# One schedule as written for the whole kernel, other PSUM banks for the turns, and a block's last products in two halves of the columns

## The chip, the cores and the metric

The kernel runs on one NeuronCore of a Trainium2 chip. Its time is device microseconds (us) of one execution; a kernel's time is the median of several. The engines are named as in the profile: PE is TensorE (PEld its weight loads), DVE VectorE, ACT ScalarE, POOL GpSimd, SP SyncE; a name with q (PEq, DVEq) is the engine's instruction queue, in which branches and loads of registers are handled. All products are matmuls on TensorE that write into PSUM, a memory of eight banks.

## The reference

Three steps follow one another. First, attention inside chunks of 64 positions, for 2 × 576 = 1152 tokens and 8 heads of 64. Second, a mixture of 8 experts in which every token goes to one expert and an expert takes at most 288 tokens. Third, a dense mixture of 4 domains.

```python
idx = argmax(x @ w_gate); gate = softmax(x @ w_gate)[idx]
# tokens of expert e in order, the first 288 kept
h = maximum(disp[e] @ w1[e], 0); y = h @ w2[e]     # 512 -> 1024 -> 512
out[i] = gate[i] * y[expert(i), place(i)]          # 0 where not kept
# dense: for each of 4 domains
out += p[:, e:e+1] * (maximum(x @ w1[e], 0) @ w2[e])
```

How many tokens an expert gets depends on the inputs; with these, six experts have tokens.

## The kernel before

**Stages.** Up to about 60 us: attention in nine tiles of 128 tokens, with the gate and the counting of places. From 60 to 240 us: the experts. From 240 to 602 us: the dense mixture. Each fp32 value is split into a high and a low part that TensorE takes at full rate; a product of two such is three matmuls (high·high, low·high, high·low; `PAIRS`). In the profile `hl` is a weight's two parts (ScalarE casts the high part, L115, VectorE subtracts to get the low one, L119), `xt` those of the tokens, `ht` those of the hidden layer.

**An expert.** The numbers that tell how many tokens each expert has are made on VectorE into the tile `ovi` at the end of attention, `gidx` holds the token numbers for the gathers, and `over` (L447) the surplus of each expert, on VectorE too. `over` is the last operation that reads the PSUM tile `n_ps`; the next stage's tiles take over the banks of attention. An expert's tokens are worked in up to three blocks, `wins`: block 0 (tokens 0 to 127), block 1 (128 to 255) and block 2, the small one, of 64 tokens. `form` says which of them are executed: 1 block 0, 2 blocks 0 and 2, 4 blocks 0 and 1, 3 all three. On every engine the blocks 1 and 2 stand in `tc.If` (L677, L682, L683), so each engine compares a register and branches. The order in an expert is block 1, the small block, block 0, and in block 0 the next expert's tokens are turned and its weights split (`also`).

With these inputs the order is, in us of the profile: first expert block 1 (from 67.9) and block 0; second block 1 (from 100.5), small block (114.7 to 126.2) and block 0; third block 0 alone (from 141.8); fourth small block (158.6 to 174.2) and block 0; fifth small block (189.6 to 206.7) and block 0; sixth block 0 alone (from 222.3).

**A block** (`block`): `first(h)` multiplies tokens by one half of `w1` into the bank `pg0[w]` or `pg1`; ScalarE copies it out (`hs`); `turn(h)` transposes it on TensorE into a tile `tp` (L580, in a small block L578); ScalarE and VectorE make `ht` of it, L596 the high and L597 the low part; `second(h)` multiplies `ht` by `w2` into `y` (L574). At the end ScalarE copies `y` to `yr` in two halves of 256 columns (L627), TensorE turns `yr` into another `tp`, and the result is split into `x2` for the dense stage. `xprep` turns the next expert's gathered tokens (L540), `xprep_small` those of its small block (L545).

**What sets the order.** In `tc.manual_schedule` an engine issues its instructions as the code is written; outside, a scheduler orders them. Before, attention is under one such context for all engines, the expert stage and the dense stage each under one of their own for four engines, and the code between them under none. A tile named `tp` comes from a pool tag of two banks that rotate (`bufs=2`): whoever writes into a bank waits for its last reader, and where that reader stands in a `tc.If`, for the engine to have passed the branch.

**Numbers in registers.** `numbers` reads values of `ovi` into a register of each engine (a `TENSOR_LOAD` in its queue, L549). Before, this happens once, ahead of the expert stage: nine values on every engine, eight more on ScalarE and VectorE.

Of the kernel before, what the change touches and what calls it, by code (L numbers as in the profile page):

```python
# [9 lines left out]
F32 = mybir.dt.float32  # L10
# [8 lines left out]
ENG = mybir.EngineType  # L19

P = 128
NTOK = 1152
# [49 lines left out]
def kernel(ctx: ExitStack, tc: tile.TileContext, kqv_d, wg, w_all, dp, cst, out, cap):  # L72
# [4 lines left out]
    assert cap <= XW  # L77

    dpool = ctx.enter_context(tc.tile_pool(name="dpool", bufs=1, space=DRAM))
    x_d = dpool.tile([NTOK, DM], F32, name="x_d")  # L80
# [44 lines left out]
    with ExitStack() as ast:  # L125
        ap_ = ast.enter_context(tc.tile_pool(name="attn", bufs=2))
        ps = ast.enter_context(tc.tile_pool(name="aps", bufs=1, space=PSUM))
        ast.enter_context(tc.manual_schedule())

# [387 lines left out]
    def w2(h, part, ff):  # L517
        return hls[2 * h + 1][:, part, ff * DM:(ff + 1) * DM]

    with ExitStack() as est, tc.manual_schedule(engines={ENG.PE, ENG.Activation, ENG.DVE, ENG.SP}):  # L520
        hp_ = est.enter_context(tc.tile_pool(name="mh", bufs=2))
        xtp = est.enter_context(tc.tile_pool(name="mx", bufs=1))
        ps = est.enter_context(tc.tile_pool(name="mps", bufs=1, space=PSUM))

        ys2 = [ps.tile([P, DM], F32, name=f"y{j}") for j in range(2)]


        pg0 = [ps.tile([P, FH], F32, name=f"pg0{j}") for j in range(3)]
        pg1 = ps.tile([P, FH], F32, name="pg1")
        xts = [xt0, xtp.tile([P, 2 * KD * XW], F32R, name="xt1")]  # L530
        xbig = [x[:, 0:4 * KD * P].rearrange("p (a k n) -> p a k n", a=2, k=KD) for x in xts]
# [16 lines left out]
        def numbers(src, **kw):  # L548
            return nc.values_load_multi_w_load_instructions(src, min_val=0, **kw)[1]  # L549

        kept, *form_r = numbers(ovi[0:1, 0:1 + NE], max_val=NTOK)
        o_r = numbers(ovi[0:1, 1 + NE:1 + 2 * NE], engines=(ENG.Activation, ENG.DVE), max_val=NTOK)
        regs = []
# [6 lines left out]
        def block(k, w, also=()):  # L560
# [4 lines left out]
            both = n < P  # L565
            y = ys2[w % 2]
            hs, ht = {}, {}
            pg = (pg0[w], pg1)

            def products(o, t, wt, start, stop):  # L570

                pairs = ((0, 0), (0, 1)) if both else PAIRS
                for i, (a, b) in enumerate(pairs):
                    nc.tensor.matmul(o, t(a), wt(b), start=start and i == 0, stop=stop and i == len(pairs) - 1)  # L574

# [15 lines left out]
            def turn(h):  # L591
                tp = ps.tile([P, NF, n], F32, tag="tp", bufs=2, name="tp")
                for j in range(NF):
                    turned(tp[:, j], hs[h][:, j * P:j * P + P])
                ht[h] = hp_.tile([P, NF, 2, n], F32R, tag="h", name="ht")
                nc.scalar.activation(out=ht[h][:, :, 0], in_=tp, func=ACTF.Relu)  # L596
                nc.vector.scalar_tensor_tensor(out=ht[h][:, :, 1], in0=tp, scalar=0.0, in1=ht[h][:, :, 0].bitcast(F32),  # L597
                                               op0=ALU.max, op1=ALU.subtract)

            def second(h, ffs):  # L600
                for j in ffs:
                    products(y, lambda a: ht[h][:, j].rearrange("p a n -> p (a n)") if both else ht[h][:, j, a],
                             lambda b: w2(h, b, j), h == 0 and j == 0, h == NH - 1 and j == NF - 1)

# [17 lines left out]
            place(4)  # L622
            second(1, range(NF))
            yr = hp_.tile([P, DM], F32, tag="ys", bufs=1, name="yr")
            ty = ps.tile([P, KD, n], F32, tag="tp", bufs=2, name="tp")
            for j in range(2):
                nc.scalar.copy(yr[:, j * 256:j * 256 + 256], y[:, j * 256:j * 256 + 256])  # L627
            place(5)
# [22 lines left out]
        def expert(k):  # L651
# [3 lines left out]
            if k == 0:  # L655
# [6 lines left out]
                for kd in range(KD):  # L662
                    xprep(0, kd, ps.tile([P, 512], F32, tag="tp", bufs=2, name="tp") if kd < 2 else (pg0[0], pg1)[kd - 2])
                for h in range(2):
# [9 lines left out]
            elif k + 2 < NE:  # L674
                gather(k + 2)
            late(k)
            with tc.If(form_r[k] > 2):  # L677
                block(k, 1)
# [20 lines left out]
            def nxt(i, kd):  # L699
                if k + 1 < NE:  # L700
                    t = pg1 if len(turns) == KD else pg0[1 + len(turns) % 2]
                    turns.append(t)
                    also[i].append(lambda: xprep(k + 1, kd, t) if kd < KD else xprep_small(k + 1, t))
# [19 lines left out]
            block(k, 0, also)  # L723
            if k == 0:
                scatter(meta_d, [(posi[:, i:i + 1], meta[:, i]) for i in range(NT)], [])
                nc.gpsimd.dma_start(out=mcol, in_=meta_d.rearrange("(i p) c -> p i c", p=P))
# [7 lines left out]

    with ExitStack() as est, tc.manual_schedule(engines={ENG.PE, ENG.Activation, ENG.DVE, ENG.SP}):
        accp = est.enter_context(tc.tile_pool(name="accp", bufs=1))
# [132 lines left out]
        def pick_last(ws):  # L869
            if len(ws) == 1:  # L870
                return dense(ws[0])
            with tc.If(kept <= LAST + ws[0]) as few:  # L872
                dense(ws[0])
            with few.Else():
                pick_last(ws[1:])
# [46 lines left out]
```

## Time and profile before

| what | value |
| --- | --- |
| median of three runs | 619.68 us (617.58, 619.68, 619.73) |
| the profiled execution | 620.28 us, of which span 618.1 us |
| TensorE busy | 579.5 us, 94% of the span |
| weight loads of TensorE (beside its matmuls) | 503.6 us, 81% |
| VectorE, ScalarE, GpSimd busy | 296.1, 200.9, 71.5 us |
| mean granted clock of TensorE | 0.975 |

The span is the time from the first to the last instruction that the profiler saw; the execution's own time is a little longer. A timeline's row is a stretch of like instructions on one engine: start, duration, engine and line, the tile written and those read, the shape, how many (x4), and in brackets how long the engine stood idle ahead of it and what it waited for. In a row of waits `A <- B` reads: A waited for B. The granted clock is a share of the full one; TensorE has the levels 1.2 and 2.4 GHz, which are 0.50 and 1.00.

### The profile page before, as it was taken

The numbers are of one execution on the slowest core, as the hardware profiler recorded it, in microseconds if no ns is written. First come the engines' busy times: TensorE is split into PE (matmuls) and PEld (weight loads), VectorE is DVE, ScalarE is ACT, GpSimd is POOL, SyncE is SP. The second block draws the span as 40 slices with busy tenths as digits, with TensorE's granted clock in tenths as the row PEclk, the third lists the DMA queues.
The fourth block names the chain that finished last, engine by engine and source line by source line (L and its number), as shares of the span: only waits on it lengthen the run. The fifth ranks groups of instructions, "written<-read, shape, count | busy, mean of one in ns | idle before, by whom it ended". The sixth has DMA issues, their size and how long they took to land.

```text
span 618.1 us, 8796 instructions
## 1 busy us (share of the span) xinstructions
PE 579.5 (94%) x3376; PEld 503.6 (81%) x3376; DVE 296.1 (48%) x576; ACT 200.9 (32%) x394; POOL 71.5 (12%) x63
## 2 busy tenths in 40 slices
PE   6998699998797988999999999999999999999995
PEld 3785577776676767989989989989989989989984
DVE  4897828147445376242462452452452452454221
ACT  4785237267454476111211211211211211211110
POOL 3311813202202050000000000000000000000032
PEclk8997799999898999999999999999999999999998
DMA  8782286428727176400120120120220000000022
GB/s 326 258 286 75 60 315 202 114 73 296 262 69 249 46 233 200 186 1 1 68 69 1 68 69 1 69 68 1 69 68 1 2 1 1 1 0 1 1 83 76
DMA packets 17322, 61.36 MB, mean 99 GB/s; under 512 B 2720, under 2 KB 2864, under 8 KB 16624
## 3 DMA queue, kind: packets, MB, share of 16 engines
q1 hardware_dynamic: 14544, 52.95, 25.1%
q0 software_dynamic: 2720, 7.66, 4.1%
q8 instruction: 33, 0.54, 0.4%
q14 instruction: 25, 0.20, 0.1%
HBM read 55.86 MB, written 4.75 MB: 98 GB/s over the span
## 4 chain that ended last, share of the span: by engine, by line
PE 59%; issue 1%; POOL 1%; DVE 0%; POOLq 0%
PE pg L768 30%; PE po L797 20%; PE po L816 8%; POOL out L500 1%; PE po L831 0%; DVE xr L804 0%; POOLq L872 0%; POOLq L500 0%
## 5 line engine op out<-in xcount | busy, mean ns | idle before, releaser
L768 PE MATMUL pg<-x,hl 128*128 128x384 f32 (+1 forms) x1152 | 187.5, 322 | 1.6 <-DVEq L728 1.6
L768 PEld LDWEIGHTS pg<-x,hl 128*128 128x128 f32 x1152 | 184.5, 188 | 3.1 <-issue 1.8
L797 PE MATMUL po<-hl,h 128*128 128x512 f32 (+1 forms) x588 | 137.4, 392 | 0.0
L797 PEld LDWEIGHTS po<-hl,h 128*128 128x128 f32 x588 | 108.6, 188 | 24.6
L119 DVE TENSOR_TENSOR hl<-raw,hl 128x1024 fp32r<-128x1024 f32 x80 | 95.3, 1219 | 24.0 <-ACT hl L115 20.2
L778 ACT ACTIVATE h<-pg 128x384 fp32r<-128x384 f32 x64 | 31.5, 492 | 186.1 <-PE pg L768 185.8
L115 ACT CAST hl<-raw 128x1024 fp32r<-128x1024 f32 x80 | 82.2, 1056 | 0.9 <-DVEq L728 0.9
L779 DVE SCALAR_TENSOR_TENSOR h<-pg,h 128x384 fp32r<-128x384 f32 x64 | 35.6, 557 | 94.2 <-ACT h L778 94.2
L574 PE MATMUL pg<-hl,xt 128*128 128x512 f32 x240 | 65.4, 421 | 3.2 <-PEq L682 1.6
L574 PE MATMUL y<-hl,ht 128*128 128x512 f32 x240 | 65.0, 412 | 1.6 <-DVE ht L597 1.6
L804 DVE SCALAR_TENSOR_TENSOR xr<-po,mcol,xr 128x512 f32<-128x512 f32 (+1 forms) x43 | 31.7, 737 | 59.7 <-PE po L797 59.0
L574 PEld LDWEIGHTS pg<-hl,xt 128*128 128x128 f32 x240 | 45.9, 200 | 14.6 <-issue 5.3
L574 PEld LDWEIGHTS y<-hl,ht 128*128 128x128 f32 x240 | 43.7, 192 | 13.4 <-DVE ht L597 4.4
L816 PE MATMUL po<-h,hl 128*128 128x288 f32 x384 | 51.9, 295 | 0.0
L816 PEld LDWEIGHTS po<-h,hl 128*128 128x128 f32 x384 | 51.3, 189 | 0.0
L775 ACT CAST h<-pg 128x288 fp32r<-128x288 f32 x32 | 12.8, 400 | 97.9 <-DVE pg L773 97.9
L400 POOL DMA_INDIRECT xr<-x_d,gidx x24 | 28.2, 1174 | 127.8 <-PE pg L540 95.4
L825 POOL MEMSET raw<- 128x512 f32 x1 | 0.5, 527 | 268.4 <-DVE hl L119 268.4
L597 DVE SCALAR_TENSOR_TENSOR ht<-tp,ht 128x512 fp32r<-128x512 f32 (+1 forms) x22 | 13.6, 616 | 28.5 <-ACT ht L596 28.4
L822 DVE TENSOR_TENSOR rest<-po,rest 128x288 f32<-128x288 f32 x28 | 12.8, 458 | 26.6 <-PE po L816 26.6
L773 DVE SCALAR_TENSOR_TENSOR pg<-pg,xt 128x288 f32<-128x288 f32 x32 | 22.1, 690 | 1.6 <-PE pg L768 1.6
L776 DVE TENSOR_TENSOR h<-pg,h 128x288 fp32r<-128x288 f32 x32 | 14.7, 459 | 15.4 <-ACT h L775 15.4
(158 smaller groups left out, 393.6 us busy)
## 6 DMA issues: line engine op xcount, KB each, us to landing
raw<-in_w_all SPq DMA_DIRECT2D x72, 512.0 KB, 4.1
kqv<-in_kqv SPq DMA_DIRECT2D x8, 768.0 KB, 8.1
raw<-in_w_all SPq DMA_DIRECT2D x4, 1024.0 KB, 5.7
x_d<-x SPq DMA_DIRECT2D x9, 256.0 KB, 3.1
xt<-meta_d SPq DMA_DIRECT2D x1, 1056.0 KB, 8.5
kqv<-in_kqv SPq DMA_DIRECT2D x3, 256.0 KB
xr<-x_d,gidx POOLq DMA_INDIRECT x24
cc<-in_cst SPq DMA_DIRECT2D x1, 373.5 KB
```

The lines of the kernel that those rows point to most:

```text
L115: nc.scalar.copy(hls[j][:, 0, a:b], raws[j][:, a:b])
L119: nc.vector.tensor_tensor(out=hls[j][:, 1, a:b], in0=raws[j][:, a:b], in1=hls[j][:, 0, a:b].bitcast(F32), op=ALU.subtract)
L400: nc.gpsimd.indirect_dma_start(out=xrs[k % 2][0:n, w, :], out_offset=None, in_=x_d[:, :], in_offset=bass.IndirectOffsetOnAxis(ap=ix, axis=0))
L574: nc.tensor.matmul(o, t(a), wt(b), start=start and i == 0, stop=stop and i == len(pairs) - 1)
L768: nc.tensor.matmul(pg[:, 0:n], w1(u % 2, a, kd)[:, ff * P:ff * P + P], x2[:, b, kd, g * GW:g * GW + n], start=c == 0, stop=c == 3 * KD - 1)
L773: nc.vector.scalar_tensor_tensor(out=hs, in0=hs, scalar=0.0, in1=domain(u // NH), op0=ALU.max, op1=ALU.mult)
L776: nc.vector.tensor_tensor(out=h[:, ff, 1, 0:n], in0=hs, in1=h[:, ff, 0, 0:n].bitcast(F32), op=ALU.subtract)
L778: nc.scalar.activation(out=h[:, ff, 0], in_=pg[:, 0:GW], func=ACTF.Relu)
L779: nc.vector.scalar_tensor_tensor(out=h[:, ff, 1], in0=pg[:, 0:GW], scalar=0.0, in1=h[:, ff, 0].bitcast(F32), op0=ALU.max, op1=ALU.subtract)
L797: nc.tensor.matmul(po, h[:, ff, a, tt * P:tt * P + P], w2(u % 2, b, ff)[:, cols], start=c == 0, stop=c == 3 * NF - 1)
L804: nc.vector.scalar_tensor_tensor(out=acc[t][:, cols], in0=po, scalar=pe, in1=acc[t][:, cols], op0=ALU.mult, op1=ALU.add)
L816: nc.tensor.matmul(po[:, 0:W], w2(u % 2, b, ff)[:, d * P:d * P + P], h[:, ff, a, 0:W], start=c == 0, stop=c == 3 * NF - 1)
```

## The change

Four things are changed, all around the expert stage.

1. `tc.manual_schedule` for TensorE, ScalarE, VectorE and SyncE now stands once, over the whole function, and over attention one for GpSimd.
2. PSUM: one `y` in place of two, and three fixed tiles `tps` in place of the rotating `tp`. The first turn of block `w` goes to `tps[w]`, the second to `pg0[w]`, the last to `tps[w]`. The next expert's tokens are turned, in the order of issue, into `pg0[1]`, `pg0[2]`, `tps[1]` (the small ones), `tps[2]` and `pg1`; before, into `pg0[1]`, `pg0[2]`, `pg0[1]`, `pg0[2]` and `pg1`.
3. `numbers`: one value is read ahead of the stage, the others one expert at a time, by `count`, behind `late(k)`; `kept` at the end of the first expert. The first expert's offset is the constant 0.
4. The last two parts of `second(1, ...)` are computed in two halves of 256 columns.

```diff
+    ctx.enter_context(tc.manual_schedule(engines={ENG.PE, ENG.Activation, ENG.DVE, ENG.SP}))
...
-        ast.enter_context(tc.manual_schedule())
+        ast.enter_context(tc.manual_schedule(engines={ENG.Pool}))
...
-    with ExitStack() as est, tc.manual_schedule(engines={ENG.PE, ENG.Activation, ENG.DVE, ENG.SP}):
+    with ExitStack() as est:
...
-        ys2 = [ps.tile([P, DM], F32, name=f"y{j}") for j in range(2)]
         pg0 = [ps.tile([P, FH], F32, name=f"pg0{j}") for j in range(3)]
+        tps = [ps.tile([P, 512], F32, name=f"tp{j}") for j in range(3)]
         pg1 = ps.tile([P, FH], F32, name="pg1")
+        y = ps.tile([P, DM], F32, name="y")
...
-        kept, *form_r = numbers(ovi[0:1, 0:1 + NE], max_val=NTOK)
-        o_r = numbers(ovi[0:1, 1 + NE:1 + 2 * NE], engines=(ENG.Activation, ENG.DVE), max_val=NTOK)
+        kept = []
+        form_r = [*numbers(ovi[0:1, 1:2], max_val=4)]
+        o_r = [0]
+        def count(k):
+            form_r.extend(numbers(ovi[0:1, 1 + k:2 + k], max_val=4))
+            o_r.extend(numbers(ovi[0:1, 1 + NE + k:2 + NE + k], engines=(ENG.Activation, ENG.DVE), max_val=NTOK))
...
             def turn(h):
-                tp = ps.tile([P, NF, n], F32, tag="tp", bufs=2, name="tp")
+                tp = (tps, pg0)[h][w][:, 0:NF * n].rearrange("p (f n) -> p f n", f=NF)
...
-            second(1, range(NF))
+            second(1, range(NF - 2))
+            halves = [slice(j * DM // 2, (j + 1) * DM // 2) for j in range(2)]
+            for cols in halves:
+                second(1, range(NF - 2, NF), cols)
             yr = hp_.tile([P, DM], F32, tag="ys", bufs=1, name="yr")
-            ty = ps.tile([P, KD, n], F32, tag="tp", bufs=2, name="tp")
-            for j in range(2):
-                nc.scalar.copy(yr[:, j * 256:j * 256 + 256], y[:, j * 256:j * 256 + 256])
+            ty = tps[w][:, 0:KD * n].rearrange("p (d n) -> p d n", d=KD)
+            for cols in halves:
+                nc.scalar.copy(yr[:, cols], y[:, cols])
...
-                    xprep(0, kd, ps.tile([P, 512], F32, tag="tp", bufs=2, name="tp") if kd < 2 else (pg0[0], pg1)[kd - 2])
+                    xprep(0, kd, (tps[0], tps[2], pg0[0], pg1)[kd])
...
             late(k)
+            if k + 1 < NE:
+                count(k + 1)
             with tc.If(form_r[k] > 2):
...
-                    t = pg1 if len(turns) == KD else pg0[1 + len(turns) % 2]
+                    t = (pg0[1], pg0[2], tps[1], tps[2], pg1)[len(turns)]
...
             block(k, 0, also)
             if k == 0:
+                kept.extend(numbers(ovi[0:1, 0:1], max_val=NTOK))
```

The lines of the new file that the text names: L448 is what L447 was, L551 what L549 was, L582 the products (L574), L586 and L588 the turns (L578, L580), L604 and L605 `ht` (L596, L597), L639 the copies to `yr` (L627), L691, L696 and L697 the branches (L677, L682, L683), L743 that to the next expert (L728).

VectorE's order at the start of the expert stage, before (from L435 `ovi` to `over`; `dt`, `tsb`, `gp` and `gidx` are the token numbers, `hl` the weights' low part):

```order
L435 TENSOR_REDUCE ovi<-pv 128x16 [waits DVE_49]
L440 TENSOR_TENSOR dt<-tsb 128x8 [waits Activation_49]
L549 TENSOR_LOAD ovi [waits DVE_49]
L918 BRANCH_PREFETCH_HINT
L441 TENSOR_TENSOR dt<-dt,thr 128x8 [waits DVE_49]
L442 TENSOR_TENSOR tsb<-tsb,dt 128x8 [waits DVE_49]
L549 TENSOR_LOAD ovi
L119 TENSOR_TENSOR hl_91<-raw_87,hl_91 128x1024 [waits DMAHW2_49]
L443 TENSOR_TENSOR gp<-tsb,sel 128x192 [waits DVE_49]
L119 TENSOR_TENSOR hl_91<-raw_87,hl_91 128x1024
L445 TENSOR_REDUCE gidx<-gp 128x24 [waits DVE_49]
L447 TENSOR_TENSOR over<-n_ps,st 128x8
```

and after:

```order
L436 TENSOR_REDUCE ovi<-pv 128x16 [waits DVE_49]
L441 TENSOR_TENSOR dt<-tsb 128x8 [waits Activation_49]
L442 TENSOR_TENSOR dt<-dt,thr 128x8 [waits DVE_49]
L443 TENSOR_TENSOR tsb<-tsb,dt 128x8 [waits DVE_49]
L444 TENSOR_TENSOR gp<-tsb,sel 128x192 [waits DVE_49]
L446 TENSOR_REDUCE gidx<-gp 128x24 [waits DVE_49]
L448 TENSOR_TENSOR over<-n_ps,st 128x8
L551 TENSOR_LOAD ovi [waits DVE_49]
L120 TENSOR_TENSOR hl_93<-raw_89,hl_93 128x1024 [waits DMAHW2_49]
L120 TENSOR_TENSOR hl_93<-raw_89,hl_93 128x1024
```

`over` has moved ahead of the two `hl` operations and of all loads, and one load stands where two stood.

TensorE's order at the start of a small block, before (`pg_1011` and `pg_1012` are the banks of `first`, `tp` the turn's):

```order
L574 MATMUL pg_1011<-hl_91,xt_1013 128x512 [waits DVE_49]
L574 MATMUL pg_1011<-hl_91,xt_1013 128x512 x7
L574 MATMUL pg_1012<-hl_93,xt_1013 128x512 [waits DVE_49,Activation_49]
L574 MATMUL pg_1012<-hl_93,xt_1013 128x512 x3
L578 MATMUL tp<-cc,hs 128x64 [waits DVE_49,Activation_49]
L578 MATMUL tp<-cc,hs 128x64 x3
L574 MATMUL pg_1012<-hl_93,xt_1013 128x512 x4
L574 MATMUL y_1007<-hl_92,ht 128x512 [waits DVE_49]
```

and after (`tp_1012` is `tps[2]`):

```order
L582 MATMUL pg_1009<-hl_93,xt_1015 128x512 [waits DVE_49]
L582 MATMUL pg_1009<-hl_93,xt_1015 128x512 x7
L582 MATMUL pg_1013<-hl_95,xt_1015 128x512 [waits DVE_49,Activation_49]
L582 MATMUL pg_1013<-hl_95,xt_1015 128x512 x3
L586 MATMUL tp_1012<-cc,hs 128x64 [waits Activation_49]
L586 MATMUL tp_1012<-cc,hs 128x64 x3
L582 MATMUL pg_1013<-hl_95,xt_1015 128x512 x4
L582 MATMUL y<-hl_94,ht 128x512 [waits DVE_49]
```

The turn's bank is a fixed one, and its wait for VectorE is no longer in the list.

TensorE's order from one expert's last turn to the next one's first product, before:

```order
L580 MATMUL tp<-cc,yr 128x128 [waits Activation_49]
L580 MATMUL tp<-cc,yr 128x128
L728 COMPARE_AND_BRANCH
L918 BRANCH_PREFETCH_HINT
L677 COMPARE_AND_BRANCH
L574 MATMUL pg_1010<-hl_91,xt_1013 128x512 [waits DVE_49]
```

and after:

```order
L588 MATMUL tp_1010<-cc,yr 128x128 [waits Activation_49]
L588 MATMUL tp_1010<-cc,yr 128x128
L743 COMPARE_AND_BRANCH
L551 TENSOR_LOAD ovi
L933 BRANCH_PREFETCH_HINT
L691 COMPARE_AND_BRANCH
L582 MATMUL pg_1008<-hl_93,xt_1015 128x512 x7
```

A load stands between the two branches.

ScalarE's order at a block's end, after:

```order
L597 COPY hs<-pg_1013 128x512 [waits DVE_49,PE_49]
L604 ACTIVATE ht<-pg_1008 128x4x128 [waits PE_49]
L639 COPY yr<-y 128x256 [waits PE_49]
L639 COPY yr<-y 128x256
L537 CAST x_995<-tp_1011 128x4x128 [waits DVE_49,PE_49,Pool_49]
```

Both copies of `y` stand behind one wait for TensorE.

## Rows read from the trace of the kernel before

**Rows 1.** Windows: busy us of each engine (instructions), granted clock, DMA share, GB/s:

```profile
65.40:72.30 6.90, 5.99 (x19) 5.08 (x20) 5.39 (x15) 1.49 (x4) 6.14 (x4) 0.51 0.10 29
114.70:126.20 11.50, 10.96 (x56) 8.36 (x56) 1.54 (x3) 3.18 (x7) 0.00 (x0) 1.00 0.07 25
139.60:158.60 19.00, 15.78 (x80) 11.80 (x77) 13.50 (x17) 13.91 (x24) 4.62 (x5) 1.00 0.88 292
158.60:174.20 15.60, 12.78 (x57) 9.74 (x57) 6.08 (x7) 4.63 (x9) 2.48 (x2) 0.89 0.59 190
189.60:206.70 17.10, 14.31 (x57) 11.14 (x57) 6.08 (x7) 4.57 (x9) 2.41 (x2) 0.80 0.53 176
240.20:602.40 362.20, 362.19 (x2089) 337.37 (x2090) 149.95 (x233) 70.38 (x125) 5.44 (x6) 1.00 0.11 37
```

**Rows 2.** TensorE's waits, 60 to 241: total us, times, longest:

```profile
PE tp L540 <- DVE over L447: 5.0, 1, 5.0
PE tp L578 <- DVEq L677: 4.5, 2, 2.3
PE tp L580 <- ACT yr L627: 2.8, 8, 0.5
PE tp L580 <- DVEq L682: 2.7, 2, 1.4
...
PE y L574 <- DVE ht L597: 1.6, 2, 1.4
```

**Rows 3.** Timeline of VectorE, 59 to 78: start, us, operation, idle before it:

```profile
59.48 0.16 DVE L440 TENSOR_TENSOR dt<-tsb 128x8 f32<-128x8 f32 x1
60.90 0.17 DVE L441 TENSOR_TENSOR dt<-dt,thr 128x8 f32<-128x8 f32 x1 [1.26 <-issue]
...
63.09 1.22 DVE L119 TENSOR_TENSOR hl<-raw,hl 128x1024 fp32r<-128x1024 f32 x1 [1.82 <-issue]
...
65.90 0.15 DVE L447 TENSOR_TENSOR over<-n_ps,st 128x8 f32<-128x8 f32 x1
67.45 0.81 DVE L536 TENSOR_TENSOR xt<-tp,xt 128x256 fp32r<-128x256 f32 x2 [1.40 <-ACT xt L535]
...
72.50 4.62 DVE L119 TENSOR_TENSOR hl<-raw,hl 128x1024 fp32r<-128x1024 f32 x4
77.03 0.68 DVE L597 SCALAR_TENSOR_TENSOR ht<-tp,ht 128x512 fp32r<-128x512 f32 x1
```

**Rows 4.** DMA activity, 57 to 63, in 40 slices of 0.15 us:

```profile
DMA  0000000000000000006774399327944696220000
```

**Rows 5.** Timeline of TensorE, 157 to 175 (a small block):

```profile
158.63 3.30 PE L574 MATMUL pg<-hl,xt 128*128 128x512 f32 x12 [0.57 <-issue]
164.21 1.76 PE L578 MATMUL tp<-cc,hs 128*128 128x64 f32 x8 [2.27 <-DVEq L677]
...
167.58 1.21 PE L574 MATMUL y<-hl,ht 128*128 128x512 f32 x4
```

**Rows 6.** Loads of numbers, L549, L364 (one number): ns of one, min/median/max:

```profile
L549 DVEq TENSOR_LOAD <-ovi x2: 1119/1500/1880, 59.6 to 61.1; - x2
...
L549 PEldq TENSOR_LOAD <-ovi x1: 1042/1042/1042, 59.6 to 59.6; - x1
...
L364 SPq TENSOR_LOAD <-e0i x1: 533/533/533, 26.7 to 26.7; - x1
```

**Rows 7.** One line's instructions on VectorE's queue, L677:

```profile
L677 DVEq COMPARE_BRANCH  x8: 43/58/163, 72.4 to 224.0; - x8
```

**Rows 8.** Timeline of VectorE, 141 to 168:

```profile
148.89 0.69 DVE L597 SCALAR_TENSOR_TENSOR ht<-tp,ht 128x512 fp32r<-128x512 f32 x1
...
159.38 4.62 DVE L119 TENSOR_TENSOR hl<-raw,hl 128x1024 fp32r<-128x1024 f32 x4
```

**Rows 9.** Waits of TensorE's weight loads, 60 to 241:

```profile
PEld pg L545 <- DVE xt L536: 0.8, 5, 0.2
```

**Rows 10.** Timeline of TensorE, 607.8 to 611.2:

```profile
607.62 3.24 PE L797 MATMUL po<-hl,h 128*128 128x512 f32 x25
```

More of the change, by code (lines that the diff above doesn't have):

```diff
@@ L565, in block @@
             both = n < P
-            y = ys2[w % 2]
             hs, ht = {}, {}
@@ L573, in products @@
                 for i, (a, b) in enumerate(pairs):
-                    nc.tensor.matmul(o, t(a), wt(b), start=start and i == 0, stop=stop and i == len(pairs) - 1)
+                    nc.tensor.matmul(o, t(a), wt(b), start=start and i == 0, stop=stop and i == len(pairs) - 1, skip_group_check=True)
             def turned(o, a):
@@ L598, in turn, with second @@
                                                op0=ALU.max, op1=ALU.subtract)
-            def second(h, ffs):
+            def second(h, ffs, cols=slice(0, DM)):
                 for j in ffs:
-                    products(y, lambda a: ht[h][:, j].rearrange("p a n -> p (a n)") if both else ht[h][:, j, a],
-                             lambda b: w2(h, b, j), h == 0 and j == 0, h == NH - 1 and j == NF - 1)
+                    products(y[:, cols], lambda a: ht[h][:, j].rearrange("p a n -> p (a n)") if both else ht[h][:, j, a],
+                             lambda b: w2(h, b, j)[:, cols], h == 0 and j == 0, h == NH - 1 and j == NF - 1)
             def place(i):
@@ L732 @@
         late(NE)
-    with ExitStack() as est, tc.manual_schedule(engines={ENG.PE, ENG.Activation, ENG.DVE, ENG.SP}):
+    with ExitStack() as est:
         accp = est.enter_context(tc.tile_pool(name="accp", bufs=1))
@@ L871, in pick_last @@
                 return dense(ws[0])
-            with tc.If(kept <= LAST + ws[0]) as few:
+            with tc.If(kept[0] <= LAST + ws[0]) as few:
                 dense(ws[0])
```

## The prediction

> **What bounds the kernel now.** I read the windows by stage first. In the dense stage TensorE is busy 362.19 of 362.20 us at a clock of 1.00 [rows 1]; the change only moves names there, so nothing is won or lost in it. What can move lies between 60 and 240 us, in the expert stage, and there the question is what TensorE waits for. The waits of TensorE answer it [rows 2]: 5.0 us once at L540 for VectorE's `over`, 4.5 in two waits of the small blocks' turn (L578) on VectorE's branch L677, 2.7 in two waits of a turn (L580) on VectorE's branch L682, 1.6 for `ht` at L574, and 2.8 in eight waits for ScalarE's copy `yr`. Then the windows again, for the clock: 0.51 in the 6.9 us behind the wait of 5.0 us. A small block that nothing disturbs (114.7 to 126.2) takes 11.5 us with TensorE busy 10.96; the same block of the fourth expert takes 15.6 (12.78 busy, clock 0.89), that of the fifth 17.1 (14.31 busy, clock 0.80) [rows 1]. So a wait of 2.27 us costs up to 5.6: the wait itself, and then matmuls at the lower of the two levels (1.2 instead of 2.4 GHz).
>
> **Entry.** VectorE's timeline tells why `over` is late: it stands idle 1.26 us before L441 and 1.82 before the first L119, each time behind a load of eight or nine numbers, and two L119 (1.22 us each) run ahead of `over`; later it idles 1.40 before L536, for the transposes that waited for `over` [rows 3]. From then it has no gap until `ht` at 77.03, for which TensorE waits. The sum of the three gaps is 4.48. After the change (the order excerpt of VectorE) L448 `over` follows the index arithmetic at once, with one load of one number behind it. I put `over` at about 60.9: 59.48 and six short operations of 0.15 to 0.17 [rows 3], the two wide ones (L443, L445) some twice that. The rows of tokens that the transposes read land up to 62.4 [rows 4], so TensorE starts about 62.4 instead of right after 65.90 + 0.15. What counts is `ht`: VectorE's same work without the 4.48 of gaps, with one load of about 0.6, makes `ht` and the first product of `y` 3.9 us earlier. Bounds: 3.4 if that load takes 1.1, as VectorE's shorter one [rows 6], and 4.2 if 0.3 of it shows. The gather is next in line, but has 1 us and more to spare behind VectorE. **−3.9.**
>
> **Small blocks.** The turn waits for VectorE's branch because the rotating bank `tp` was last read inside a block that this expert skips. VectorE gets to that branch only behind four L119 (159.38, 4.62 us, to 164.00 [rows 8]), and TensorE starts at 164.21 [rows 5]. The turn now has the bank `tp2`, and in the order its only wait is that for ScalarE. If both blocks become like the undisturbed one, this gives 4.1 + 5.6 = 9.7. What is late next is `ht`'s low half, on VectorE behind the same four L119: 164.0 + 0.4. Without its wait the turn would start at 161.9; from turn to `y` there are 3.4 us at the lower clock (164.21 to 167.58), some 1.9 at the full one, so `y` at 163.9 and a new wait of about 0.5. The load priced below (0.8) delays TensorE past it and takes its place, so I don't count both. **−9.7**, bounds −9.7 and −4.5 (the waits go, the clock falls all the same).
>
> **Single-block experts.** Here the wait on L682 (1.38 and 1.35) goes too, but `ht` was bound by VectorE itself: L119 ends and `ht` starts at 148.89 without a gap [rows 8], and VectorE's order there is the same. TensorE gets 1.1 us of slack and only 0.3 each as time. **−0.6**, and the load in front of these two experts is hidden in that slack.
>
> **Small transposes.** L545 waited 0.8 us in five for VectorE's reading of `pg0` [rows 9]; now they write `tp1`. **−0.6** (0 to −0.8).
>
> **Loads.** The two big loads went away from the entry, where TensorE was idle, and each engine now loads one number in each expert (ScalarE and VectorE two), and once more for `kept`. On TensorE's queue this stands between an expert's last turn and its first product, where TensorE's queue was already last: 0.57 idle at 158.63 with nothing to wait for [rows 5]. So its whole duration shows. One number took SyncE's queue 0.533 us, nine took TensorE's 1.042 [rows 6]; no row shows one number on TensorE. I take 0.8, the middle, since both ends are equally near. Of six loads two lie ahead of the second expert, one each ahead of the third to sixth; the two of the single-block experts are hidden, four show: 3.2 (2.1 to 4.2), less 0.2 of a wait for `ht` that two of them cover. **+3.0.** On VectorE and ScalarE the loads stand behind four L119 or two casts, and their sequencers run ahead: VectorE's queue had the branch L677 at 72.4, when the four L119 ahead of it were only beginning (72.50, 4.62 us) [rows 3, 7]. There I charge nothing; the third rival has the price without that cover. SyncE and GpSimd load one number more, between the triggers of weights and gathers that are wanted a block later: nothing.
>
> **Halves.** Six products of 512 columns become twelve of 256 (four become eight in a small block). The 25 products at 607.62 are one of 512 columns and 24 of 256 [rows 10]: with 0.234 for the first and 0.28 for the last one's run, 23 steps take 2.73, 0.119 each, so two cost 0.237 against 0.234 of a whole. Six times 0.003 is 0.02 us a block. **+0.2** in eleven blocks (0 to 0.4). Nothing comes back for it: in ScalarE's order the first half's copy still waits for TensorE's last product, since both halves lie in one bank, and the second copy waits for nothing. The Trainium skill, "PSUM — Partial Sum Buffer", section "PSUM bank collisions raise a hardware error", bears on this: a bank has to be guarded as a whole, since accesses of two engines to disjoint columns collide too. By it the copy can't start while the second half is written and the halves give nothing; without it they would give what the second rival says. The order sides with the page.
>
> **Sum.** −3.9 − 9.7 − 0.6 − 0.6 + 3.0 + 0.2 = −11.6 us.
>
> **The clock.** The removed stalls are replaced by shorter ones: TensorE would reach its first `y` some 3 us before `ht` at the entry, and the pauses between experts grow by a load. After a wait of 2.27 us in a block the clock fell twice; the stretch with a change of expert and a wait of 1.38 kept 1.00 (139.6 to 158.6) [rows 1, 2]. I charge one fall at the price that the fourth expert's block paid in TensorE's busy time, 12.78 − 10.96: **+1.8**. The Trainium skill, "TensorE: Matmul & The Clock Gate", section "Why this matters for your kernels", speaks against the change here: idle between bursts of matmuls brings the clock back down. The rows agree where the pause was long. With a fall at every lengthened pause its rule makes the first rival.
>
> Total −9.8 on the profiled execution's 620.28 us, of which 618.1 are span and 2.2 lie around it and stay: 610.5. The median of the three runs lies 0.6 lower (619.68), so I forecast **609.9**.
>
> **Rivals.** *First: the clock falls at the entry and ahead of each of the five later experts*, six falls of 1.8, and the four loads take 1.04: −11.6 + 1.0 + 10.8 = +0.2, so 619.9, no change. For it: 2.27 us was enough twice. Against: a change of expert left the clock at 1.00 [rows 1], and transposes run in it. 0.08.
>
> *Second: the copy of the first half does run beside the second half's products.* Then most of the wait for `yr`, 2.8 in eight [rows 2], goes as well: 609.9 − 2.8 = 607.1. Against it: the one bank and the single wait. 0.06.
>
> *Third, slower: the loads on VectorE do not run ahead.* Two loads then stand between the four L119 and `ht` in each of six experts; at 1.12 to 1.88 us each [rows 6], 3.0 a pair, TensorE's `y` comes 18 us later in all: 609.9 + 18 = 627.9. It decides from 1.6 us a pair, where the −9.8 are used up. For it: at the entry the loads left VectorE idle for 1.26 and 1.82 [rows 3]. Against: there only short operations stood ahead of them, here four L119, past which the branch was taken up [rows 7]. 0.04.
>
> *Fourth: the turn's new bank still hangs on VectorE*, because a bank that also takes the next expert's transposes (`tp1`, `tp2`, `pg0`) is read by VectorE. The 9.7 are then lost, and two of the loads hide: 609.9 + 9.7 − 1.6 = 618.0, within 0.5%. Against: the order lists a wait for ScalarE alone. 0.05.
>
> **Chances and range.** My forecast 0.77, with a range of its own of 606.5 to 615 (loads ±1, entry ±0.5, none to three falls, small blocks part of the way). 0.5%, 3.1 us, is about what a measurement can tell from no change, so faster means below 616.6. The forecast and the second rival lie below it but for a tail of 0.02; the first and fourth are no change, with 0.01 of each beyond either side; the third is slower. Faster 0.82, same 0.13, slower 0.05. Range 605.5 to 617.0.
>
> **What would show it.** Right: no wait of TensorE on a branch of VectorE in the expert stage; the small blocks at 11.5 to 12.3 us; the transposes at about 62.4 and `ht` at about 73; one load row of 0.5 to 1 us on TensorE's queue at each change of expert; waits for `yr` unchanged. Wrong: `ht` still at 75 or later, granted clock near 0.5 in several stretches after 75 us, or gaps of VectorE ahead of `ht` in every expert.

## The result, and the profile after

The changed kernel takes 610.95 us (median of four runs, 606.49 to 611.23) against 619.09 for the kernel before on the same chip (617.58 to 619.73): a ratio of 0.9855, 95% interval 0.9806 to 0.9905. Six more runs on another chip gave 611.35, ratio 0.9859 (0.982 to 0.9898). The profiled execution took 611.23 us with a span of 609.5, against 620.28 and 618.1. I had forecast 609.9, with a range of 605.5 to 617.0.

**Where the time went.** The two spans can be cut at the same events: the product `n_ps` that ends attention, the start of each block's last turn (`yr`), and the first dense product. All columns are differences of such starts in us, read from the timelines of TensorE; "expert stage" runs from the first block's last turn to the first dense product, "4th, 5th small" are the small blocks of the fourth and fifth expert with the change of expert ahead of them, "3rd, 6th" the single blocks with theirs. "ht" is the time from `n_ps` to the first `ht` on VectorE. The last column is the span, which is given to 0.1 us, less the others.

| kernel | attention | ht | entry, to the first turn of yr | ahead of 2nd, with its block 1 | 4th small | 5th small | 3rd | 6th | expert stage | dense to the end |
| --- | --- | --- | --- | --- | --- | --- | --- | --- | --- | --- |
| before | 56.42 | 20.61 | 27.94 | 14.04 | 15.91 | 17.49 | 16.99 | 17.19 | 155.85 | 377.89 |
| after | 55.95 | 16.63 | 25.46 | 14.50 | 13.36 | 13.36 | 16.57 | 16.72 | 148.87 | 379.22 |
| all numbers at once behind the splitting (e1) | 55.50 | 16.78 | 24.10 | 14.14 | 13.34 | 13.36 | 16.58 | 16.74 | 148.47 | 377.93 |
| no halves (e2) | 55.81 | 17.15 | 24.48 | 14.62 | 13.32 | 13.33 | 16.56 | 16.69 | 148.67 | 379.83 |
| turning banks (e3) | 56.22 | 17.09 | 24.44 | 14.54 | 17.51 | 15.96 | 17.03 | 17.19 | 156.72 | 377.92 |
| surplus late (e4) | 56.07 | 17.58 | 24.90 | 14.50 | 13.35 | 13.35 | 16.54 | 16.72 | 148.70 | 379.13 |
| all numbers ahead (e5) | 54.88 | 18.94 | 26.27 | 14.13 | 13.35 | 13.35 | 16.59 | 16.73 | 148.44 | 378.01 |
| fill (e6) | 59.14 | 16.56 | 23.90 | 14.52 | 13.36 | 13.34 | 16.84 | 16.74 | 149.11 | 378.04 |
| low half later (e7) | 56.42 | 14.86 | 22.17 | 14.50 | 13.33 | 13.33 | 16.54 | 16.72 | 148.70 | 377.81 |
| two banks for y (e8) | 60.43 | 16.76 | 25.15 | 14.51 | 13.03 | 13.04 | 16.39 | 16.51 | 146.24 | 378.18 |
| banks alone (e11) | 59.16 | 20.61 | 27.92 | 13.98 | 13.34 | 13.35 | 16.54 | 16.76 | 148.17 | 378.05 |

From before to after: attention −0.47, entry −2.48, expert stage −6.98, dense stage +1.33; together −8.60, the difference of the spans. Another 0.45 of the 9.05 lies outside the span, which takes 1.7 us there instead of 2.2; no run shows why. The expert stage repeats within some 0.2 us from execution to execution, where nothing is changed in it (148.87 and 148.79 for the changed kernel; only e6 has one pause of 0.70 more, in the third expert). "ht" repeats less well: kernels whose VectorE does the same up to it have 16.5 to 17.2. Attention repeats worst: it took 54.9 to 60.4 in these profiles, though each engine's operations in it are the same, in the same order. The dense stage takes 377.8 to 378.2 or 379.1 to 380.2 by whether the clock falls at its start. So a kernel's single times spread over some 5 us, and parts of 1 us are read from the table, not from medians. The median of e9 below is that of five runs; a sixth, 613.99 us, lies over 1.5% above its fastest and is left out as a slow one.

TensorE's waits between 55 and 235 us of the kernel after (total us, times, longest):

```profile
PE y L582 <- DVE ht L605: 4.3, 4, 2.1
PE pg L582 <- PEq L691: 3.3, 3, 1.2
PE tp L588 <- ACT yr L639: 2.8, 8, 0.5
PE tp L542 <- DMA xr<-x_d,gidx: 1.9, 2, 1.1
PE pg L783 <- DVEq L743: 1.6, 1, 1.6
PE tp L586 <- ACT yr L639: 1.6, 3, 0.5
```

TensorE's waits on VectorE's `over` and on its two branches [rows 2] are gone. In their place stands a wait for `ht` (L605), 4.3 us in four, and one of 1.9 for the gathered tokens. That for `yr` (L639) is 2.8 in the eight large blocks, as before, and 1.6 in the three small ones, which [rows 2] does not show:

```profile
PE tp L578 <- ACT yr L627: 1.6, 3, 0.5
```

So it is 4.4 in all eleven, before and after.

VectorE's timeline at the entry, after (start, duration, operation, idle before it):

```profile
60.35 0.15 DVE L448 TENSOR_TENSOR over<-n_ps,st 128x8 f32<-128x8 f32 x1
60.76 2.36 DVE L120 TENSOR_TENSOR hl<-raw,hl 128x1024 fp32r<-128x1024 f32 x2 [0.25 <-issue]
63.25 0.76 DVE L538 TENSOR_TENSOR xt<-tp,xt 128x256 fp32r<-128x256 f32 x2
...
72.58 0.68 DVE L605 SCALAR_TENSOR_TENSOR ht<-tp,ht 128x512 fp32r<-128x512 f32 x1
```

`over` is at 60.35, 5.55 earlier than in [rows 3]; of the three gaps one of 0.25 is left, for a load of one number; `ht` starts 4.45 earlier, 3.98 if counted from `n_ps`. TensorE's timeline there:

```profile
62.43 0.55 PE L542 MATMUL tp<-cc,xr 128*128 128x128 f32 x3 [1.08 <-DMA xr<-x_d,gidx]
...
69.32 1.63 PE L582 MATMUL pg<-hl,xt 128*128 128x512 f32 x6
70.80 0.40 PE L582 MATMUL y<-hl,ht 128*128 128x512 f32 x1
73.32 2.50 PE L582 MATMUL y<-hl,ht 128*128 128x512 f32 x5 [2.13 <-DVE ht L605]
```

It now waits for the gathered tokens (1.08) and then 2.13 for `ht`. Behind that wait its five products take 2.50 us, where six (69.32) took 1.63. The windows of the kernel after (busy us of each engine, granted clock, DMA share, GB/s) show the fall:

```profile
73.30:76.50 3.20, 3.18 (x10) 2.59 (x11) 0.00 (x0) 0.00 (x0) 2.17 (x3) 0.50 0.83 302
112.40:123.90 11.50, 10.98 (x60) 8.71 (x61) 1.54 (x3) 3.18 (x7) 0.00 (x0) 1.00 0.01 3
156.50:168.90 12.40, 11.04 (x61) 8.77 (x61) 5.57 (x7) 3.83 (x8) 1.78 (x2) 1.00 0.76 252
184.70:197.30 12.60, 10.99 (x61) 8.71 (x61) 5.77 (x7) 4.03 (x8) 1.98 (x2) 1.00 0.76 232
230.30:233.70 3.40, 3.40 (x11) 3.40 (x12) 2.96 (x3) 1.99 (x2) 0.79 (x1) 0.52 0.39 125
```

0.50 at 73.3 to 76.5, and 0.52 at the start of the dense stage, where the kernel before had 1.00 in its first 5 us behind the same wait of 1.6. The three small blocks are alike in TensorE's work now (10.98, 11.04, 10.99 us at 1.00) where [rows 1] had 10.96, 12.78, 14.31. The fourth expert's small block on TensorE, ScalarE and VectorE:

```profile
156.52 3.08 PE L582 MATMUL pg<-hl,xt 128*128 128x512 f32 x12 [1.19 <-PEq L691]
159.44 1.05 PE L586 MATMUL tp<-cc,hs 128*128 128x64 f32 x8
...
162.29 1.20 PE L582 MATMUL y<-hl,ht 128*128 128x512 f32 x4 [0.82 <-DVE ht L605]
```

```profile
161.39 0.39 ACT L604 ACTIVATE ht<-tp 128x256 fp32r<-128x256 f32 x1 [2.06 <-DVEq L691]
```

```profile
156.59 4.62 DVE L120 TENSOR_TENSOR hl<-raw,hl 128x1024 fp32r<-128x1024 f32 x4
161.81 0.42 DVE L605 SCALAR_TENSOR_TENSOR ht<-tp,ht 128x256 fp32r<-128x256 f32 x1 [0.59 <-ACT ht L604]
```

The turn at 159.44 waits for nothing. But `y` waits 0.82 for `ht`, and behind that stands the old wait in another place: ScalarE's half of `ht` (L604) now stands idle 2.06 us until VectorE, past its four L120 (to 161.21), signals at the branch L691 that the skipped block is behind it (its queue had compared the register at 158.8 already); it starts at 161.39, and VectorE's half waits 0.59 for it. The two halves so run one after the other behind the four L120. In the fifth expert it is the same:

```profile
ACT ht L604 <- DVEq L691: 4.4, 2, 2.3
```

The likely reason is that `ht` itself comes from a pool of two buffers that rotate (tag `h` in `turn`), whose last user stands in the skipped block; no run gave it fixed buffers. And the loads (ns, min/median/max) are short:

```profile
L551 DVEq TENSOR_LOAD <-ovi x14: 300/306/555, 60.1 to 215.0; - x14
...
L551 PEldq TENSOR_LOAD <-ovi x8: 298/308/486, 59.2 to 211.7; - x8
```

0.308 us is the median on TensorE's queue, against 1.042 for nine numbers [rows 6] and the 0.8 that I took.

### The profile page after: what moved, and what is told of

The parts are those of the page before. It is cut to its first block, busy times and chain, and to the rows that moved or that the text cites. A ratio compares the mean times of both kernels' runs of the same rounds, so it can differ in the third digit from the quotient of the medians.

```text
span 609.5 us, 8953 instructions
## 1 busy us (share of the span) xinstructions
PE 576.9 (95%) x3436; PEld 505.3 (83%) x3436; DVE 296.2 (49%) x576; ACT 200.5 (33%) x394; POOL 70.5 (12%) x63
## 4 chain that ended last, share of the span: by engine, by line
PE 60%; issue 1%; POOL 0%; POOLq 0%; DVE 0%
PE pg L783 30%; PE po L812 21%; PE po L831 8%; POOL out L501 0%; PE po L846 0%; POOLq L933 0%; DVE xr L819 0%; POOLq L887 0%; POOLq L501 0%
## 5 line engine op out<-in xcount | busy, mean ns | idle before, releaser
L120 DVE TENSOR_TENSOR hl<-raw,hl 128x1024 fp32r<-128x1024 f32 x80 | 95.2, 1220 | 22.4 <-ACT hl L116 20.0
L582 PE MATMUL y<-hl,ht 128*128 128x512 f32 (+1 forms) x300 | 66.0, 365 | 4.4 <-DVE ht L605 4.3
L582 PE MATMUL pg<-hl,xt 128*128 128x512 f32 x240 | 62.5, 408 | 5.8 <-PEq L691 3.3
L582 PEld LDWEIGHTS y<-hl,ht 128*128 128x128 f32 x300 | 47.9, 191 | 15.4 <-DVE ht L605 8.6
L582 PEld LDWEIGHTS pg<-hl,xt 128*128 128x128 f32 x240 | 44.6, 193 | 16.2 <-issue 7.3
L597 ACT COPY hs<-pg 128x512 f32<-128x512 f32 x22 | 12.9, 588 | 24.5 <-PE pg L582 19.0
```

Source lines behind the costliest of these rows:

```text
L120: nc.vector.tensor_tensor(out=hls[j][:, 1, a:b], in0=raws[j][:, a:b], in1=hls[j][:, 0, a:b].bitcast(F32), op=ALU.subtract)
```

## The experiments

Each is the changed kernel with one edit, if not told otherwise, timed in five rounds against the kernel before; the ratios are to that.

**The base again.** 

> The changed kernel once more, as the base of the others of this set. Both theories expect 610.9 us, with single runs between 606 and 611.5 as so far, the shorter ones at a higher mean clock.

611.35 us (608.1 to 615.49). In its profile attention took 59.32 us, the clock fell at the entry and at the dense stage as in the first, and the expert stage was the same within 0.1. These are the six further runs of the section above.

**e1, the price of the loads.**

```diff
-            if k + 1 < NE:
-                count(k + 1)
+            if k == 0:
+                nums = numbers(ovi[0:1, 0:1 + NE], max_val=NTOK)
+                kept.append(nums[0]); form_r.extend(nums[2:])
+                o_r.extend(numbers(ovi[0:1, 2 + NE:1 + 2 * NE], engines=(ENG.Activation, ENG.DVE), max_val=NTOK))
...
-                kept.extend(numbers(ovi[0:1, 0:1], max_val=NTOK))
```

> All numbers are read at once behind the first expert's weight splitting, none at the later changes of expert. Theory (the one-number loads stand in the open on TensorE's queue at the changes of expert, 0.3 to 0.6 us each, while on VectorE the large loads hide behind four splitting operations): 608.7 us (607.7 to 609.5), pauses ahead of the second to fifth expert shorter by 0.3 to 0.8. Rival (their time is hidden, the pauses grew for another reason): no change, 610.9.

610.27 us, ratio to before 0.986 (0.9825 to 0.9895): no difference to the changed kernel, and outside the theory's 607.7 to 609.5. The pauses did get shorter, as the theory says, but the time did not. TensorE in the fourth expert's small block of e1:

```profile
153.60 3.35 PE L577 MATMUL pg<-hl,xt 128*128 128x512 f32 x12 [0.47 <-issue]
...
160.08 1.21 PE L577 MATMUL y<-hl,ht 128*128 128x512 f32 x4 [1.31 <-DVE ht L600]
```

The pause at the change of expert is 0.47 instead of 1.19, and the wait for `ht` 1.31 instead of 0.82. The stage is as long as before the edit (13.34 and 13.36). Only ahead of the second expert, where `ht` is not late, 0.36 is won. So the loads cost 0.4 us in all. Both theories were half right: the pauses come from the loads, and most of them are hidden.

**e2, the halves.**

```diff
-            second(1, range(NF - 2))
+            second(1, range(NF))
             halves = [slice(j * DM // 2, (j + 1) * DM // 2) for j in range(2)]
-            for cols in halves:
-                second(1, range(NF - 2, NF), cols)
```

> The last products of a block in whole columns again. Theory (one bank, both copies wait for the last product, so the halves cost 0.02 us a block and give nothing): 610.7, within 0.3 of the changed kernel. Rival (the first half's copy runs beside the second half's products): slower by about 2.8, 613.7, with longer waits for the copy of y.

609.67 us, ratio 0.9841 (0.9808 to 0.9874). The expert stage is 0.20 shorter, 0.02 or so a block, as priced, but no more than the stage repeats within; the wait for `yr` is still 2.8 in eight and 1.5 in three. The median is 1.3 under the changed kernel's, more than the theory has, but within the spread of the runs. The rival is out.

**e3, the banks.**

```diff
-                tp = (tps, pg0)[h][w][:, 0:NF * n].rearrange("p (f n) -> p f n", f=NF)
+                tp = ps.tile([P, NF, n], F32, tag="tp", bufs=2, name="tp")
...
-                    t = (pg0[1], pg0[2], tps[1], tps[2], pg1)[len(turns)]
+                    t = pg1 if len(turns) == KD else pg0[1 + len(turns) % 2]
...
```

The last turn and the first expert's tokens go back into the rotating `tp` in the same way.

> The turns in two rotating banks and the next expert's tokens in pg0 as before, all else as changed. Theory (the fixed banks alone take the small blocks' wait on VectorE's branch away): two waits of about 2.3 us come back, each with a fall of the clock, and some 0.7 at the single-block experts: 618 us (616 to 620). Rival (the order and the loads gave that too): at most 612.

614.34 us, ratio 0.9925 (0.9897 to 0.9953). Its waits of TensorE, 55 to 240 us:

```profile
PE tp L585 <- DVEq L690: 4.2, 2, 2.3
...
PE tp L587 <- DVEq L695: 2.0, 2, 1.0
```

Both waits on VectorE's branches are back. The expert stage is 156.72, 7.85 longer, nearly all of it in the four stages of the table. The median is below the range that the theory gave, 616 to 620: it is 3.0 to 3.4 over the changed kernel's two medians, not 7. In the profile the two waits are 4.2 and the clock falls behind both (0.52 from 161 to 168, 0.51 from 195.4 to 198.9); whether it does so in the other runs was not traced. The wait for `ht` in the small blocks, which the changed kernel has instead, is gone here, so that part of the 4.2 is no loss.

**e11, the other way round**: the kernel before with the new banks and nothing else.

```diff
-        ys2 = [ps.tile([P, DM], F32, name=f"y{j}") for j in range(2)]
+        y = ps.tile([P, DM], F32, name="y")
+        tps = [ps.tile([P, 512], F32, name=f"tp{j}") for j in range(3)]
...
-                tp = ps.tile([P, NF, n], F32, tag="tp", bufs=2, name="tp")
+                tp = (tps, pg0)[h][w][:, 0:NF * n].rearrange("p (f n) -> p f n", f=NF)
...
```

The last turn, the first expert's tokens and those of the next expert get the changed kernel's banks too.

> The kernel before with nothing changed but the PSUM banks (fixed ones for the turns, one y). Theory (the banks alone shorten the two small and the two single-block stages, by 7.8 in the profile, and the entry stays as it was with its 27.9 us): 611.5 (610 to 614). Rival (the banks need the new order or the late numbers to have an effect): 617 or more.

613.17 us, ratio 0.9901 (0.9862 to 0.9939), against 619.76 for the kernel before in the same set. The entry is as before to 0.02, the expert stage 7.68 shorter, with the small blocks at 13.34 and 13.35. The banks need neither the order nor the late numbers, and e3 and e11 enclose their share: 7.7 to 7.9 us of the profile. In the medians it is 3.0 to 3.4 (e3) and 6.6 (e11), so most of what the change gives in time comes from the banks, and how much of it is less sure than the profile makes it look.

**e4 and e5, the two causes at the entry.** In e4 the two splitting operations stand ahead of `over` again; in e5 all numbers are read ahead of the stage again.

```diff
+        part_lo(0, 0)
         nc.vector.tensor_tensor(out=gp, in0=bc(tsb, NE, 1), in1=bc(sel, 3, 2), op=ALU.mult)
+        part_lo(0, 1)
...
-                for h in range(2):
-                    part_lo(0, h)
```

> VectorE's two first splitting operations ahead of the surplus again, as before the change, with the one load of one number behind it. Theory (at the entry the two large loads cost the time, not the place of the surplus, since the gathered rows land late anyway): the first ht 0.5 to 0.8 us later, 611.6. Rival (the place of the surplus gave the entry's 4 us): ht 2.4 us later and more, 613.5 or more.

```diff
-        form_r = [*numbers(ovi[0:1, 1:2], max_val=4)]
-        o_r = [0]
+        nums = numbers(ovi[0:1, 0:1 + NE], max_val=NTOK)
+        kept.append(nums[0]); form_r = nums[1:]
+        o_r = [0] + list(numbers(ovi[0:1, 1 + NE:1 + 2 * NE], engines=(ENG.Activation, ENG.DVE), max_val=NTOK))[1:]
...
```

`count`, its calls and the late reading of `kept` go with it.

> All numbers read at once ahead of the stage, as before the change, in the new order of VectorE. Theory (at that place VectorE stands idle for both loads, nearly 3 us, and ht follows): ht at about 75.3 instead of 72.6, against some 2 us less at the later changes of expert: 611.5 (610.5 to 612.5). Rival (the loads are cheap wherever they stand): 608.7.

611.12 (ratio 0.9882, 0.9848 to 0.9916) and 611.11 us (0.9882, 0.9846 to 0.9917). The medians can't tell them from the base; `ht` can: 17.58 after `n_ps` in e4, 0.95 later than after the change, 18.94 in e5, 2.31 later. VectorE's timeline of e4 has the gap of 1.4 ahead of L538 (here L540) again, that of e5 the gap of the loads:

```profile
64.04 0.81 DVE L540 TENSOR_TENSOR xt<-tp,xt 128x256 fp32r<-128x256 f32 x2 [1.39 <-ACT xt L539]
```

```profile
62.19 2.36 DVE L120 TENSOR_TENSOR hl<-raw,hl 128x1024 fp32r<-128x1024 f32 x2 [2.82 <-issue]
```

Of the 3.98 us by which the change makes `ht` earlier, the loads have some 2.3, the place of `over` 0.95, and the rest is where both meet. Since `ht` lies at 16.5 to 17.2 without either edit, these are 1.8 to 2.4 and 0.4 to 1.1. In the whole time this is small: the entry of e5 is only 0.81 longer than that of the changed kernel's profile, in which the clock fell, and 0.4 comes back in the expert stage.

**e6, the pause and the clock.**

```diff
+            if k == 0 and w == 1:
+                for j in range(8):
+                    nc.tensor.matmul(tps[0], xbig[0][:, 0, j % KD, lo:lo + n], w1(0, 0, j % KD), start=True, stop=True)
             second(0, (0, 1))
```

> Eight products into a bank that nobody reads, in TensorE's pause ahead of the first y. Theory (that pause of 2.1 us lets the clock fall behind it): clock 1.00 between 73 and 77, 1.6 us less, 609.3. Rival (the clock falls there for another reason, or elsewhere instead): 610.9.

609.49 us, ratio 0.9845 (0.9818 to 0.9872). In the profile of e6 TensorE's `y` and the window behind it:

```profile
72.65 1.98 PE L628 MATMUL tp<-hl,xt 128*128 128x512 f32 x8
...
76.43 1.44 PE L582 MATMUL y<-hl,ht 128*128 128x512 f32 x5 [1.57 <-DVE ht L605]
```

```profile
76.50:80.00 3.50, 3.50 (x17) 2.78 (x18) 0.69 (x1) 0.60 (x1) 2.59 (x4) 1.00 0.92 295
```

The clock stayed at 1.00, and from `ht` to the first turn of `yr` it took 7.34 us instead of 8.83: the 1.5 that a fall costs there. But that does not prove the cause. In e1, e3, e4 and e11 the pause was 2.0, 2.7, 2.8 and 2.4 us long without any fill, and the same stretch took 7.3. Of the seven profiles with an unfilled pause of 2 us or more there, three show the fall (after, its repetition, e8) and four don't. So a fall can follow such a pause and need not, and the length of the pause does not decide between the two. What does is open.

**e7, what is late next at the entry.**

```diff
-            with tc.If(form_r[k] > 2):
-                block(k, 1)
+            with tc.If(form_r[k] > 2) as two:
+                block(k, 1, () if k else ((), (), (lambda: part_lo(3, 0), lambda: part_lo(3, 1)), (), (), (), ()))
             if k == 0:
+                with two.Else():
+                    for h in range(2):
+                        part_lo(3, h)
+                for h in range(2):
+                    load(1, 3, h)
```

`late` leaves these operations out for the first expert.

> In the first expert the low half of the last weights is made behind the first ht instead of ahead of it. Theory (what is late next at the entry is VectorE's splitting ahead of ht): ht and the first y 2.3 us earlier, no pause there and so no fall of the clock: 3.9 less, 607.0. Rival (another wait takes its place, the weights' low part in the second layer): 610 or more.

607.75 us, ratio 0.9834 (0.9795 to 0.9873). `ht` came 1.77 earlier, the entry was 3.29 shorter (1.5 of it the fall of the clock, which is not there), and TensorE waits for it 0.31 instead of 2.13:

```profile
72.01 1.43 PE L582 MATMUL y<-hl,ht 128*128 128x512 f32 x5 [0.31 <-DVE ht L605]
```

What bounds the changed kernel's entry is VectorE's splitting ahead of `ht`.

**e8, two banks for `y`.** All products of `y` in halves, the first in the bank `y0`, the second in that of the first turn, which `ht` has left by then; `cut` holds the two slices of columns.

```diff
+            y = (y0, tps[w][:, 0:DM // 2])
...
+                    for c in cs:
+                        products(y[c], lambda a: ht[h][:, j].rearrange("p a n -> p (a n)") if both else ht[h][:, j, a],
+                                 lambda b: w2(h, b, j)[:, cut[c]], h == 0 and j == 0, h == NH - 1 and j == NF - 1)
...
-            ty = tps[w][:, 0:KD * n].rearrange("p (d n) -> p d n", d=KD)
+            ty = pg0[w][:, 0:KD * n].rearrange("p (d n) -> p d n", d=KD)
...
-                nc.scalar.copy(yr[:, cols], y[:, cols])
+                nc.scalar.copy(yr[:, cut[c]], y[c])
```

> The two halves of y in two banks, all of its products in halves of 256 columns. Theory (in one bank the copy can't start beside the products; in two it can): the waits for the copy, 4.4 us in eleven blocks, shrink by 0.3 each, 0.05 a block goes into the smaller products: 608.4. Rival (the copy is late for another reason, its own start or the two copies in a row): no gain, 611.5.

607.37 us, ratio 0.9803 (0.9771 to 0.9835). TensorE's wait for `yr` between 60 and 240 us, and ScalarE's timeline at the end of the second expert's block 0:

```profile
PE pg L588 <- ACT yr L642: 0.2, 1, 0.2
```

```profile
140.62 0.38 ACT L642 COPY yr<-y 128x256 f32<-128x256 f32 x1
141.26 0.37 ACT L642 COPY yr<-tp 128x256 f32<-128x256 f32 x1 [0.27 <-PE tp L582]
```

The first copy (140.62) runs beside the last products of the other half, and of 4.4 us of waits 0.2 are left; nine blocks are 0.1 to 0.4 shorter, the expert stage 2.63; where the rest of the 4.2 went was not traced. So the halves are worth their cost in two banks and not in one. This is what the Trainium skill, "PSUM — Partial Sum Buffer", section "PSUM bank collisions raise a hardware error", says of a bank: it has to be guarded as a whole, so that a copy out of one half has to wait for the writes to the other. The waits agree, with 4.4 us in one bank and 0.2 in two; they are waits of the program's own, and no run here reads a bank while it is written.

**e9 and e10, together.** e9 joins e1, e2 and e7, e10 joins e1, e7 and e8; each edit stands above.

> Numbers read at once behind the first splitting, the last weights' low half behind the first ht, no halves. Theory: the sum of the three, 2.0 + 3.9 + 0.2 less than the changed kernel, 604.8 (603 to 606.5). Rival (they share one cover): 607 or more.

606.43 us, ratio 0.9809 (0.9761 to 0.9856), at the upper end of the theory's range: the entry 22.57, the expert stage 148.10. In the profile the entry is 2.9 shorter than the changed kernel's (3.3 in e7 alone) and the expert stage 0.8 (0.4 in e1 and 0.2 in e2 alone). So the terms nearly add up, but e1's is only 0.4 of the 2.0 expected.

> The two banks for y, the numbers read at once, and the last weights' low half behind the first ht, in one kernel. Theory (they act at different places: 2.6 us at the blocks' ends, 0.4 ahead of the second expert, 3.3 at the entry, read from the profiles of each alone): 6.3 less than the changed kernel, 604.7 (603 to 606.5). Rival (they share a cover): 606.5 or more.

609.3 us, ratio 0.983 (0.9802 to 0.9857), slower than the theory's range and in the rival's, though not for the rival's reason. The entry (22.04) and the blocks add up as expected: 6.6 us less than the changed kernel up to the last turn of `yr`. Then a wait at the start of the dense stage takes 2.8 of it back:

```profile
PE pg L787 <- ACTq L747: 4.2, 1, 4.2
```

ScalarE's queue takes 4 us over the branch at the end of the last expert (L747), in place of less than 1 in the other kernels, and the clock falls behind it. Why that branch is slow in this program was not found. None of the versions that were run is clearly better than e8: e7, e8 and e9 took 607.75, 607.37 and 606.43, and their intervals overlap.

## Why the prediction was right, by its steps

The forecast was 609.9, the measured median 610.95, and the sum on the profile −9.8 against −9.05. Most of the mechanisms were right; some terms were off, and partly cancelled each other. That the sum came within 0.8 us is in part luck. The expert stage gave 0.7 less than its terms, the entry with its fall of the clock 0.4 more. What I had put down as unchanged came to +0.4: attention −0.47, the dense stage +1.33, the time outside the span −0.45.

- **Entry, −3.9.** `ht` came 3.98 us earlier, and the second of the waits for the gathered rows ended at 62.43 where I had 62.4 for the transposes; one of them ran at 61.05. e4 and e5 show the two causes, of which the loads are the larger (1.8 to 2.4 against 0.4 to 1.1).
- **The clock, +1.8.** One fall at the entry, 1.5 us (8.83 against 7.34 from `ht` to `yr`). A second of 1.3 came at the start of the dense stage, which I had put down as unchanged. That the change makes it is not shown: of the 14 profiles, with the same code there, six have it, five of them behind a pause of 1.55 us that six others have without a fall; the kernel before and e3 have 1.6 and no fall.
- **Small blocks, −9.7, with 1.6 of the loads set against it.** The two stages gave 2.55 + 4.13 = 6.7 instead of 8.1. TensorE's waits and the falls are gone, by the banks, as e3 and e11 show. The step that was mis-sized is the one on what is late next: I had `ht` 0.5 us late and hidden by a load of 0.8. With the load in front it is still 0.82 and 1.09 late. I had the low half start as VectorE's four L119 end, as if the high half were ready by then. But ScalarE's high half waits for VectorE's branch too (L691, 2.06 and 2.33 us) and only then starts, and the low half waits 0.59 for it. That wait was in none of my terms; it costs at most the 0.59, and no run took it away.
- **Loads, +3.0.** Measured 0.4, the term that was furthest off. A load of one number took 0.308 us on TensorE, and where I let four of them show, only those ahead of the second expert do (e1); in front of the small blocks `ht` is later anyway.
- **Single-block experts, −0.6.** 0.42 and 0.47, so −0.9.
- **Small transposes, −0.6.** Nothing: block 0 of the second, fourth and fifth expert took 15.02, 15.03 and 14.92 and takes 15.04, 15.04 and 14.92. I had counted the weight loads' wait [rows 9] as if it stood in TensorE's matmuls, and it did not.
- **Halves, +0.2.** 0.2 (e2), as much as the stage repeats within.

The second rival fell with e2 (no gain by the halves), and e8 shows what it would have needed; its price of 2.8 left out the three small blocks, with which the wait is 4.4. The third did not happen: VectorE's two loads (157.9 and 158.4 in the fourth expert) lie under its four L120. The fourth did not either: in the expert stage TensorE waits for no branch of VectorE. ScalarE does, at `ht`, which no rival had. The first had falls at every lengthened pause; none came at a change of expert, one at the entry.

## What to carry to other kernels

A PSUM bank that rotates past a conditional block ties its next writer to the other engine's branch, even where the block is skipped; a fixed bank by block removes that. Look for every such tile on the path: here `ht` was left, and ScalarE's wait for the same branch took over part of TensorE's. Before a stall is priced, ask who else is late at the same place: here the small blocks stopped at VectorE's `ht`, which stood behind its weight splitting, so neither the removed wait nor the added load had its full size. Split a result for an early copy only if the parts lie in different banks.

## What the runs showed of the hardware

- A load of one number from SBUF into an engine's register took 0.27 to 0.31 us (medians by engine 0.278 to 0.308), of nine 1.04 on TensorE [rows 6], 0.87 in e1.
- With the same code and data, attention took 54.9 to 60.4 us; the difference goes with the granted clock in its first 35 us (0.67 to 1.00 over the stretch from 10 to 20 us in these profiles). Over the runs of all kernels 0.01 of mean clock goes with 4.8 us of time (a straight line through the runs, one level for each kernel).
- After pauses of 2.0 to 2.8 us at the same place the clock fell in some profiles and not in others. The Trainium skill, "TensorE: Matmul & The Clock Gate", section "Why this matters for your kernels", warns of idle between bursts of matmuls; behind these pauses the clock fell in three profiles of seven.
